# K^T V per head in 64-column tiles of TensorE instead of head pairs on the whole array

## The chip, the cores and the metric

The kernel runs on one core of a Trainium2 chip. The metric is device time of one execution in microseconds; the time before is the median of five runs, 145.91 us (145.01 to 146.12). TensorE multiplies matrices (in the profile PE for its matmuls and PEld for its weight loads), VectorE is DVE, ScalarE is ACT, GpSimd is POOL, and SyncE is SP, which here issues the loads and nearly all stores.

## What is computed

A gated linear attention is followed by a maxout feed-forward layer. In the reference, cut to what matters:

```python
batch, n_heads, seq, head_dim = (4, 8, 768, 48)
for t in range(S):
    state = alpha[:, :, t, :, None] * state + np.einsum('bhd,bhe->bhde', k[:, :, t], v[:, :, t])
    y[:, :, t] = np.einsum('bhd,bhde->bhe', q[:, :, t], state)
x = y.transpose(0, 2, 1, 3).reshape(B * S, H * D)     # 3072 tokens of 384
out = np.maximum(x @ w1, x @ w2) @ w_out              # d_ff = 1024
```

Inputs and output are float32. Each head's state is a 48 x 48 matrix.

## The kernel before

The sequence is cut into chunks of 128 steps, and two chunks of one batch element (256 tokens, all 8 heads) make a unit: 12 units, u = 0 to 11. Unit u works on batch element u % 4, so the state that unit u starts from comes from unit u - 4. Inside a chunk the recurrence is turned into matmuls. `ln` takes the logarithm of alpha on ScalarE (L193), `sumd` and `sumc` form running sums by matmul (L223, L237), `expm`, `expp` and `expd` exponentiate them, `kmul` and `qmul` scale k and q with the result into fp16 tiles `kn` and `qn` (L285 on GpSimd, L289 on VectorE). These tiles give each head 64 columns, of which 48 hold data and 16 are zero. `turn` transposes kn and qn (L296, evacuated at L303); `pmm` forms the scores of each head (L345, tile `pp`), `pmask` masks them (L351, tile `pt`); `ystate` and `yin` add the state's part and the chunk's own part of y (L369, L381); `xturn` transposes y (L397). The feed-forward part of a unit runs one unit later: `hid` (L410, relu at L415) and `outx`, `outg` (L429, L435, evacuated at L439). It uses max(a, b) = b + relu(a - b), with w1 - w2 and w2 times w_out formed once near the start. `dummies` (L504) are matmuls on zeros in the first part.

The change is in two small functions. `kvmm(u, cc)` forms K^T V of chunk cc for all heads on TensorE. It takes a pair of heads at a time: the 128 columns of two heads of kn are the stationary operand, and the 96 columns of the same two heads of v are streamed (L318). The result in PSUM is 128 x 96 for each pair, of which only the two 48-column blocks on the diagonal are wanted. Units 0 and 1 (`PAIRED`) keep the steps of a chunk in half of the partitions, and need two matmuls of 64 rows that add up (L312). `kvsum(u, cc)` then adds the decayed state `sb` to the two wanted blocks on VectorE, one half of the partitions at a time (L331), or copies them where no state exists yet (L333). Its result `tm` goes to `state`, where GpSimd multiplies it with the decay into the next `sb` (L277).

The instructions' order on each engine is written by hand (`manual_schedule`), and each engine runs its queue in order. For units 2 to 11 the loop body orders TensorE's work so:

```python
kvmm(u, 0); pmm(u, 0)          # then kvsum, pmask, state on other engines
if more(u): kvmm(u, 1)         # u + 4 < 12, so units 2 to 7
hid(u - 1, 0); hid(u - 1, 1); sumd(u + 1); hid(u - 1, 2); sumc(u + 1)
pmm(u, 1); ystate(u); hid(u - 1, 3, True)
outp(u - 1, 0); yin(u); turn(u + 1, 0); turn(u + 1, 1)
outx(u - 1, 1); xturn(u); outg(u - 1, 1)
```

The work ahead of a unit's first kvmm is thus `outg` (L435) of the unit before. Loads of unit u + 4 stand at the head of the body on SyncE's queue, in buffers of four.

Of the kernel before, what the change touches and what calls it, by code (L numbers as in the profile page):

```python
# [9 lines left out]
FP32 = mybir.dt.float32  # L10
# [5 lines left out]
def kernel(  # L16
# [27 lines left out]
    nc = tc.nc  # L44
    B, H, S, D = q.shape
    C = 128
    HP = H // 2
# [7 lines left out]
    PAIRED = (0, 1)  # L55
# [63 lines left out]
    for n in range(2):  # L119
        f = slice(n * NF // 2, (n + 1) * NF // 2)  # L120
        nc.sync.dma_start(out=wof[:, f], in_=moe_w_out.rearrange("(s p) d -> p s d", p=128)[:, f])  # L121
    for n in range(4):
        f = slice(n * DFF // 4, (n + 1) * DFF // 4)
# [8 lines left out]
    for cc in range(2):  # L132
        r = slice(64 * cc, 64 * cc + 64)
        for j in range(2):
            nc.gpsimd.affine_select(
                out=mc[r, j], in_=mc[r, j], compare_op=ALU.is_ge, fill=0.0, base=-j,
                pattern=[[1, 2], [2, 64]], channel_multiplier=-2,
            )
        r = slice(64 * cc, 64 * cc + 32)
# [4 lines left out]
    for cc in range(2):  # L144
        r = slice(64 * cc, 64 * cc + 64)
# [19 lines left out]
    for j in range(2):  # L165
        r = slice(64 * j, 64 * j + 64)
        nc.gpsimd.affine_select(
            out=um[r], in_=um[r], compare_op=ALU.is_ge, fill=0.0, base=-j,
# [14 lines left out]
    def pair(t, j):  # L183
        return t[:, 2 * j : 2 * j + 2, :].rearrange("p h w -> p (h w)")

    def new(tag, shape, dtype, bufs, name):
        return psp.tile(shape, dtype, tag=tag, bufs=bufs, name=name)


    def ln(u):  # L190
        X = st[u]
        X["lg"] = LG[u % NB]
        nc.scalar.activation(  # L193
            out=X["lg"][:, :, :, 0:D], in_=X["af"].rearrange("p h j d -> p j h d"), func=ACTF.Ln
        )

    def vcast(u):
        X = st[u]

        X["v16"] = gp.tile([128, 3, H, D], FP16, tag="v16", name="v16")  # L200
        for cc, j in ((0, 0), (1, 1), (0, 1), (1, 0)):
            o = X["v16"][64 * j : 64 * j + 64, cc]
            i = X["vf"][64 * cc : 64 * cc + 64, :, j, :]
            if cc == j:
                nc.gpsimd.tensor_copy(out=o, in_=i)  # L205
            else:
                nc.scalar.copy(out=o, in_=i)  # L207
                if u in PAIRED:
                    nc.gpsimd.tensor_copy(out=X["v16"][64 * cc : 64 * cc + 64, 2], in_=i)
# [93 lines left out]
            nc.vector.tensor_copy(out=X["qk"][:, cc], in_=tp.rearrange("p n h t -> p (n h) t"))  # L303

    def kvmm(u, cc):
        X = st[u]
        X["kvp", cc] = kvp = new(f"g{3 - cc}", [128, HP, 2 * D], FP32, 1, "kv")
        for j in range(HP):
            if u in PAIRED:
                r = slice(64 * cc, 64 * cc + 64)  # L310
                for i in range(2):
                    nc.tensor.matmul(  # L312
                        kvp[:, j, :], lhsT=pair(X["kn"][i][r], j),
                        rhs=X["v16"][r, cc if i == cc else 2, 2 * j : 2 * j + 2, :],
                        start=(i == 0), stop=(i == 1),
                    )
            else:
                nc.tensor.matmul(  # L318
                    kvp[:, j, :], lhsT=pair(X["kn"][cc], j), rhs=X["v16"][:, cc, 2 * j : 2 * j + 2, :],
                    start=True, stop=True,  # L320
                )

    def kvsum(u, cc):
        X = st[u]
        tm = X[f"tm{cc}"] = gp.tile([128, HP, D], FP32, tag=f"tm{cc}", bufs=6 if cc else 3, name="tm")
        kvp = X["kvp", cc]
        for a in range(2):
            r = slice(64 * a, 64 * a + 64)
            e = slice(D * a, D * a + D)
            if ("sb", cc) in X:  # L330
                nc.vector.tensor_add(out=tm[r], in0=kvp[r, :, e], in1=X["sb", cc][r])  # L331
            else:
                nc.vector.tensor_copy(out=tm[r], in_=kvp[r, :, e])  # L333

    def more(u):
        return u + B < NU
# [190 lines left out]
    dummies(1)  # L527
    wturn(0)
    kvmm(0, 0)
    kvmm(0, 1)  # L530
    kvsum(0, 0)
    state(0, 1)
    load(2)
    pmm(0, 1)
    pmask(0, 1)
    kvsum(0, 1)
    dummies(2)
    wturn(1)
# [41 lines left out]
    ln(2)  # L580
    outp(0, 0)
    kvmm(1, 0)
    kvmm(1, 1)
    kvsum(1, 0)
    state(1, 1)
    kvsum(1, 1)
# [102 lines left out]
```

## Time and profile before

| | |
|---|---|
| median of five runs | 145.91 us (145.01 to 146.12) |
| the profiled execution | 146.12 us, span 144.4 us |
| granted TensorE clock | 1.00 |
| TensorE busy | 134.8 us (93%), 1689 matmuls |
| weight loads | 97.0 us (67%), 1689 |
| ScalarE, VectorE, GpSimd busy | 96.6 (67%), 87.5 (61%), 56.6 us (39%) |
| HBM | 23.59 MB read, 4.72 MB written, 196 GB/s over the span |
| matmuls of kvmm | 64 of 128x96 (L318), 32 of 64x96 (L312) |
| VectorE operations of kvsum | 32 adds (L331), 8 copies (L333), 64x192 each |

A busy time is the sum over instructions of one engine within the span. Matmuls are pipelined, and the profile gives each of them its whole latency (206 ns for a kv matmul of 96 columns), so their spacing is read from the chain of waits: it follows the work that ended last back from the end, and gives each piece the time from its start to the start of the next. A line of the chain reads: start in us, length in us, engine, tile and line, number of instructions. A line of a group reads: line, engine, operation, out<-in, shapes and number, then busy us and mean ns, then the engine's idle time before it and what ended it.

### The profile page before, as it was taken

The page shows a single profiled execution, that of the slowest core. Times are in us where ns is not written, and L with a number is a line of the kernel's source. Part 1 is how long each engine was busy: PE and PEld are TensorE (multiplying, and loading weights), DVE is VectorE, ACT ScalarE, POOL GpSimd, SP SyncE. Part 2 cuts the span into 40 slices and gives each one's busy share as a digit, 9 for nine tenths or more (in the row PEclk, how much of TensorE's full clock was granted, in tenths as well). Part 3 has the DMA queues.
Part 4 walks back from the last instruction along what each step waited for, and adds up shares of the span by engine and source line. Part 5 has one row for each costly group of instructions (what it writes and reads, how often), then busy time and mean ns, then how long its engine had stood idle before and what let it go on. Part 6 is the DMA issues. An engine that isn't in the chain of part 4 may idle for free.

```text
span 144.4 us, 4259 instructions
## 1 busy us (share of the span) xinstructions
PE 134.8 (93%) x1689; PEld 97.0 (67%) x1689; DVE 87.5 (61%) x180; ACT 96.6 (67%) x200; POOL 56.6 (39%) x111
## 2 busy tenths in 40 slices
PE   6868879998999999999999999999999999999991
PEld 2335545755867677777877777678777777776770
DVE  6048883855966757765767777566676765671110
ACT  3467732498587686789686976786869767655530
POOL 7491542056424346173191371641913716410000
PEclk9999999999999999999999999999999999999999
DMA  4999999969959979999799999979959979020203
GB/s 113 270 371 309 305 368 346 241 126 211 198 102 250 138 142 300 159 216 186 160 293 140 283 202 215 241 133 269 197 97 294 207 136 370 0 109 5 109 0 109
DMA packets 76483, 28.58 MB, mean 198 GB/s; under 512 B 71728, under 2 KB 74672, under 8 KB 76464
## 3 DMA queue, kind: packets, MB, share of 16 engines
q1 hardware_dynamic: 76320, 28.22, 86.0%
q8 instruction: 13, 0.21, 0.7%
q10 hardware_dynamic: 144, 0.10, 0.2%
q14 instruction: 6, 0.05, 0.1%
HBM read 23.59 MB, written 4.72 MB: 196 GB/s over the span
## 4 chain that ended last, share of the span: by engine, by line
PE 64%; SPq 22%; DMA 8%; ACT 2%; issue 1%; DVE 0%; ACTq 0%
PE hp L410 19%; PE op L435 17%; SPq L75 10%; DMA af<-in_alpha_dram 8%; PE op L429 7%; SPq L85 5%; PE tp L296 5%; PE pp L345 3%; SPq L124 3%; PE cs L237 3%; PE ya L381 2%; PE xp L397 2%; PE kv L318 2%; SPq L115 2%; SPq L121 1%
## 5 line engine op out<-in xcount | busy, mean ns | idle before, releaser
L410 PE MATMUL hp<-xt,w 128*128 128x256 f16 x288 | 37.7, 273 | 0.7 <-ACT outs L439 0.2
L415 ACT ACTIVATE gT<-hp 128x512 f16<-128x512 f32 x47 | 27.9, 597 | 14.8 <-PE hp L410 14.3
L351 DVE TENSOR_TENSOR pt<-pp,um 128x512 f16<-128x512 f32 x48 | 30.9, 686 | 10.7 <-PE pp L345 10.4
L435 PE MATMUL op<-wo,gT 128*128 128x384 f16 x184 | 34.0, 326 | 0.0
L285 POOL TENSOR_TENSOR kn<-kf,Em 128x384 f16<-128x384 f32 x24 | 23.4, 996 | 25.7 <-ACT Em L247 25.7
L410 PEld LDWEIGHTS <-w 128*128 128x128 f16 x288 | 25.9, 97 | 5.9 <-issue 1.4
L435 PEld LDWEIGHTS <-gT 128*128 128x128 f16 x184 | 17.5, 98 | 10.5
L277 POOL TENSOR_TENSOR sb<-tm,dd 128x192 f16<-128x192 f32 x20 | 10.1, 506 | 30.9 <-DVE tm L331 22.9
L289 DVE TENSOR_TENSOR qn<-qf,cs 128x384 f16<-128x384 f32 x24 | 12.3, 551 | 12.8 <-ACT de L257 11.9
L439 ACT COPY outs<-op 128x384 f32<-128x384 f32 x23 | 10.9, 476 | 13.0 <-PE op L435 12.9
L331 DVE TENSOR_TENSOR tm<-kv,sb 64x192 f32<-64x192 f32 x32 | 11.3, 353 | 8.8 <-PE kv L318 7.9
L205 POOL CAST v<-vf 64x384 f16<-64x384 f32 x24 | 12.0, 501 | 9.0 <-DMA vf<-in_v_dram 8.0
L303 DVE COPY qk<-tp 128x1024 f16<-128x1024 f16 x20 | 12.9, 686 | 4.3 <-PE tp L296 4.3
L429 PE MATMUL op<-w2o,xt 128*128 128x384 f16 x69 | 15.0, 326 | 0.0
L193 ACT ACTIVATE lg<-af 128x768 f16<-128x768 f32 x12 | 10.1, 843 | 6.1 <-DMA af<-in_alpha_dram 5.9
L207 ACT CAST v<-vf 64x384 f16<-64x384 f32 x24 | 12.2, 510 | 2.5 <-DMA vf<-in_v_dram 2.0
L247 ACT ACTIVATE Em<-cs 128x384 f32<-128x384 f32 x24 | 11.6, 485 | 2.5 <-PE cs L237 2.5
L252 ACT ACTIVATE cs<-cs 128x384 f32<-128x384 f32 x24 | 11.8, 494 | 0.0
L504 PE MATMUL warm<-wz 128*128 128x512 f16 x30 | 9.9, 442 | 1.3 <-DVE halves L149 1.3
L388 ACT CAST xn<-ya 128x384 f16<-128x384 f32 x24 | 10.4, 492 | 0.0
L296 PE MATMUL tp<-ident,kn 128*128 128x128 f16 x96 | 9.3, 218 | 1.0 <-DVE qn L289 0.5
L345 PE MATMUL pp<-qk 48*128 48x128 f16 x192 | 9.8, 217 | 0.4 <-DVE qk L301 0.4
(66 smaller groups left out, 155.2 us busy)
## 6 DMA issues: line engine op xcount, KB each, us to landing
af<-in_alpha_dram SPq DMA_DIRECT2D x12, 384.0 KB, 5.7
vf<-in_v_dram SPq DMA_DIRECT2D x12, 384.0 KB, 4.7
out_dram<-outs SPq DMA_DIRECT2D x11, 384.0 KB, 4.4
kf<-in_k_dram SPq DMA_DIRECT2D x40, 96.0 KB, 4.6
qf<-in_q_dram SPq DMA_DIRECT2D x40, 96.0 KB, 4.0
w2f<-in_moe_w_dram SPq DMA_DIRECT2D x3, 512.0 KB, 5.9
wof<-in_moe_w_out_dram SPq DMA_DIRECT2D x2, 768.0 KB, 8.2
w1f<-in_moe_w_dram SPq DMA_DIRECT2D x4, 384.0 KB, 9.3
```

Source lines behind the costliest of these rows:

```text
L75: nc.sync.dma_start(out=t[name].rearrange("p h j d -> p h (j d)"), in_=rows(src, u, 0, 2 * C).rearrange("h (p j) d -> p h (j d)", j=2),)
L207: nc.scalar.copy(out=o, in_=i)
L285: nc.gpsimd.tensor_mul(out=X["kn"][cc][:, :, 0:D], in0=part(u, "kf", cc), in1=X["Em"][cc])
L289: nc.vector.tensor_mul(out=X["qn"][cc][:, :, 0:D], in0=part(u, "qf", cc), in1=X["csv"][cc])
L296: nc.tensor.transpose(tp[:, n, j, :], pair(src, j), ident)
L303: nc.vector.tensor_copy(out=X["qk"][:, cc], in_=tp.rearrange("p n h t -> p (n h) t"))
L345: nc.tensor.matmul(pa[a][:, j, :], lhsT=qk[r, 1, j, :], rhs=qk[r, 0, j, :], start=True, stop=True)
L351: nc.vector.tensor_mul(out=pt[:, a], in0=X["pa", cc][a], in1=um.unsqueeze(1).to_broadcast([128, HP, C]))
L410: nc.tensor.matmul(hp[:, n, :], lhsT=w12[:, ds, f * 128 : (f + 1) * 128], rhs=X["xt"][:, ds].rearrange("p n t -> p (n t)"), start=(ds == 0 ...
L415: nc.scalar.activation(out=gT[:, 2 * f2 : 2 * f2 + 2, :], in_=hp, func=ACTF.Relu)
L429: nc.tensor.matmul(op, lhsT=X["xt"][:, ds, n, :], rhs=w2o[:, ds, :], start=(ds == 0), stop=False)
L435: nc.tensor.matmul(op, lhsT=X["gT"][:, f, n * C : (n + 1) * C], rhs=wo16[:, f, :], start=False, stop=(f == NF - 1))
```

## The change

Each head gets its own matmul: the 64 columns of kn of one head are stationary, the 48 columns of v of the same head are streamed. The result of an even head goes to PSUM partitions 0 to 63, that of an odd head to 64 to 127, side by side in a tile of 64 columns of the array each. The PSUM tile has 48 instead of 96 columns for a pair, and holds only wanted values, so that one VectorE operation over 128 partitions takes the place of two over 64.

```diff
-        X["kvp", cc] = kvp = new(f"g{3 - cc}", [128, HP, 2 * D], FP32, 1, "kv")
+        X["kvp", cc] = kvp = new(f"g{3 - cc}", [128, HP, D], FP32, 1, "kv")
         for j in range(HP):
-            if u in PAIRED:
-                r = slice(64 * cc, 64 * cc + 64)
-                for i in range(2):
+            for i in range(2 if u in PAIRED else 1):
+                for a in range(2):
+                    h = 2 * j + a
+                    if u in PAIRED:
+                        r = slice(64 * cc, 64 * cc + 64)
+                        lhsT, rhs = X["kn"][i][r, h, :], X["v16"][r, cc if i == cc else 2, h, :]
+                    else:
+                        lhsT, rhs = X["kn"][cc][:, h, :], X["v16"][:, cc, h, :]
                     nc.tensor.matmul(
-                        kvp[:, j, :], lhsT=pair(X["kn"][i][r], j),
-                        rhs=X["v16"][r, cc if i == cc else 2, 2 * j : 2 * j + 2, :],
-                        start=(i == 0), stop=(i == 1),
+                        kvp[64 * a : 64 * a + 64, j, :], lhsT=lhsT, rhs=rhs,
+                        start=(i == 0), stop=(i == 1 or u not in PAIRED),
                     )
-            else:
-                nc.tensor.matmul(
-                    kvp[:, j, :], lhsT=pair(X["kn"][cc], j), rhs=X["v16"][:, cc, 2 * j : 2 * j + 2, :],
-                    start=True, stop=True,
-                )
...
         tm = X[f"tm{cc}"] = gp.tile([128, HP, D], FP32, tag=f"tm{cc}", bufs=6 if cc else 3, name="tm")
-        kvp = X["kvp", cc]
-        for a in range(2):
-            r = slice(64 * a, 64 * a + 64)
-            e = slice(D * a, D * a + D)
-            if ("sb", cc) in X:
-                nc.vector.tensor_add(out=tm[r], in0=kvp[r, :, e], in1=X["sb", cc][r])
-            else:
-                nc.vector.tensor_copy(out=tm[r], in_=kvp[r, :, e])
+        if ("sb", cc) in X:
+            nc.vector.tensor_add(out=tm, in0=X["kvp", cc], in1=X["sb", cc])
+        else:
+            nc.vector.tensor_copy(out=tm, in_=X["kvp", cc])
```

## Prediction

> **What bounds the kernel now.** I began with the page's busy table, then the chain of waits in order of time, then the busy time by stretches, then the groups of the lines that the change touches. The busy table and one stretch:
>
> ```profile
> PE 134.8 (93%) x1689; PEld 97.0 (67%) x1689; DVE 87.5 (61%) x180; ACT 96.6 (67%) x200; POOL 56.6 (39%) x111
> 78.00:88.00 10.00, 10.00 (x145) 7.66 (x142) 6.94 (x14) 7.75 (x17) 4.28 (x8) 1.00 1.06 210
> ```
>
> The columns of the second line are the stretch, its length, PE, PEld, DVE, ACT and POOL busy with counts, the clock, DMA share and GB/s. TensorE is busy throughout, at clock 1.00, while VectorE works 6.94 of 10 us. A busy TensorE need not be a full one, so the chain has to say whether it waits (start, us, engine and line):
>
> ```profile
> 87.54 0.17 PE kv L318 x4
> 87.71 0.33 PE pp L345 x8
> 88.03 0.28 PE kv L318 x4
> 88.31 1.31 PE hp L410 x12
> 89.62 0.18 PE cs L223 x8
> 89.80 0.68 PE hp L410 x6
> 90.47 0.43 PE cs L237 x4
> 90.91 0.23 PE pp L345 x8
> 91.13 0.20 PE ya L369 x16
> 91.33 0.76 PE hp L410 x6
> ...
> 93.88 0.40 PE ya L381 x16
> ...
> 97.30 0.17 PE kv L318 x4
> 97.47 0.33 PE pp L345 x8
> 97.80 1.42 PE hp L410 x12
> ```
>
> Each piece starts where the one before ends. From 49.79 us to the last evacuation at 141.30 the chain is TensorE alone but for one 0.61 us activation near the end. One unit with two kv groups lasts 97.30 - 87.54 = 9.76 us. So a change in TensorE's own time counts in full there, and VectorE time does not. Earlier it is different:
>
> ```profile
> ACT lg L193 <- DMA af<-in_alpha_dram: 5.9, 5, 2.4
> 48.50:58.00 9.50, 9.32 (x124) 7.01 (x119) 6.64 (x13) 7.31 (x16) 4.33 (x8) 1.00 0.92 197
> ```
>
> Until 48.53 us the chain runs through SyncE's DMA issues and the landings of alpha. The logarithms start at 39.27, 48.53 and 58.26 us, each after a wait for alpha; the one at 48.53 holds the next activation back, and TensorE stands still for 0.3 us until 49.79. Waits for alpha end with the one at 58.26.
>
> **VectorE part.** Forty half-height operations become twenty full ones. The rows:
>
> ```profile
> L331 DVE TENSOR_TENSOR tm<-kv,sb 64x192 f32<-64x192 f32 x32 | 11.3, 353 | 8.8 <-PE kv L318 7.9
> L289 DVE TENSOR_TENSOR qn<-qf,cs 128x384 f16<-128x384 f32 x24 | 12.3, 551 | 12.8 <-ACT de L257 11.9
> ```
>
> From 192 to 384 elements the time rises by 198 ns, about 1.03 ns an element; 128 more elements (the 128x512 pt at 686 ns) add 135 ns, the same slope. The 64-partition row lies on the line of the 128-partition rows, so height is free and the new operation should take the same 0.35 us. Twenty times 0.353 = 7.1 us leave VectorE. On the path this is worth nothing after 49.79 us, since no TensorE piece there waits for tm or for the pt that follows it; the state product on GpSimd, which does wait for tm, is ready 0.35 us sooner and waits longer for its next input. Before that TensorE waits once for tm (0.3 us at L369), but the next logarithm waits for alpha anyway. I cost it at zero; uncovered, that wait would return 0.3 us.
>
> **TensorE part: which groups are on the path.** The 16 unpaired kv groups are two in each unit 2 to 7 and one in each unit 8 to 11. Those of units 2 and 3 (starts 37.74 to 48.61 us) lie ahead of the stand before 49.79 us, whose 0.3 us can cover them. Units 4 to 11 start at 58.02 and later: 4 x 2 + 4 x 1 = 12 groups count.
>
> **TensorE part: the stream.** A group is now 4 matmuls of 96 columns, 0.17 us (42 ns each). It becomes 8 of 48 columns, with 8 weight loads of 64 columns instead of 4 of 128. No row shows column tiles. Lower bound: L369 runs 48-column matmuls two at a time in two row tiles, 16 in 0.20 us, so 8 in 0.10, or -0.07 us a group. If the two column tiles do not overlap, L381 is the row: 48-column matmuls on the whole array, 16 in 0.40 us, so 8 in 0.20, or +0.03. Above that, a weight load may be left in the open. All loads in the trace have 128 columns and are recorded at 92 to 98 ns, hidden behind matmuls at their best. Exposed once per pair they give 4 x 0.097 = 0.39 us, +0.22; exposed one by one 8 x 0.097 = 0.78, +0.61. The nearest row is L369 (two tiles, the same 48 columns), but its loads are of the wide kind, so I move away from it and take 0.17 us: no gain, no loss in the stream. Twelve groups: 0, between 12 x -0.07 = -0.84 and 12 x 0.22 = +2.6 us, at the very worst 12 x 0.61 = +7.3.
>
> The Trainium skill, "TensorEngine Tiling (Array Packing)", Restrictions, says that column tiling disables the fast weight load, and "TensorE: Matmul & The Clock Gate", LDWEIGHTS, gives a load as its columns divided by 1.2 in ns; as an estimate from that page 64 columns are 53 ns, hence 0.21 us a group with the tiles' loads side by side, and the total would be 0.5 us above mine, while its Part 3 promises overlap of column tiles. No run here shows a narrow load.
>
> **TensorE part: changing the array's shape.** This is the term that the diff does not show. The page's forms give L345, L369 and L237 48 or 64 rows, the others 128. Wherever the chain passes between the kinds, a piece is longer than its twin that comes from its own kind: pp after the full-height kv 0.33 against 0.23 after cs (+0.10); kv after pp 0.28 against 0.17 (+0.11); hp x12 after pp 1.42 against 1.31 after kv (+0.11); hp x6 after ya 0.76 against 0.68 (+0.08). So 0.10 us a change of shape. The Trainium skill, "TensorEngine Tiling (Array Packing)", Key Properties, says that changing the tiling mode drains the array, which agrees with these 0.08 to 0.11 us for row tiles; no run here shows it for columns.
>
> In the built instruction order the kv matmuls carry tiles of 128 rows by 64 columns, at columns 0 and 64. In a two-group unit the order is op, kv, pp, kv, hp. Before, op to kv and kv to hp were the same shape; the two changes were around pp. After, all four borders change shape: two more. In units 8 to 11 (op, kv, pp, hp) only op to kv is new: one more. On the path 4 x 2 + 4 x 1 = 12 additional changes. Bounds: 0 if column tiles change shape freely; 0.11, the dearest row, if they are like row tiles; I take 0.10, because the same array has to empty. 12 x 0.10 = +1.2 us. Units 0, 2 and 3 have 1 + 2 + 2 = 5 more changes, under the alpha loads; without that cover +0.5 us.
>
> **Waits and queues.** No wait moves: the orders of ScalarE, GpSimd and SyncE are unchanged, VectorE's only merges pairs, and the kv matmuls keep their place. What is behind a slower kv group is everything on TensorE; what is behind a faster tm is the pt operation, off the path. No DMA is added.
>
> **Sum.** VectorE 0, stream 0, shape +1.2 us. The profiled execution took 146.12 us, of which 144.4 is span and 1.7 lies around it; it becomes 147.3. It was the slowest of the five runs, 0.2 above the median of 145.91, so the median should come to 147.1, +0.8%.
>
> **Rivals.** *The pairs pay and the change of shape is free (faster).* If two column tiles run as L369's row tiles do (0.10 us) and a border to a column tile costs nothing, the sum is -0.84 us: 145.1, -0.6%. For it: L369 and L345 really run in pairs. Against it: four independent borders in the chain cost 0.08 to 0.11 us. It decides once the border costs under 0.01 us with pairs at 25 ns each; with borders at 0.07 the two cancel. *Narrow loads in the open (much slower).* With one exposed load per pair, +2.6 + 1.2 = +3.8: 149.7. For it: no row shows a load of 64 columns. Against it: TensorE hides nearly all loads today, and the row-tile pairs keep 25 ns. *It does nothing that can be seen.* If pairs gain 0.07 and borders cost 0.10, the net is 12 x 0.03 = +0.4 us, 146.3. *VectorE's release matters:* only before 49.79 us, at most the 0.3 us named above.
>
> **How the numbers follow.** A measurement of this kernel can tell about 0.5%, 0.73 us, from no change. My forecast, borders at 0.10 and a stream within 0.05 us of today's a group, has 0.52; its own range is 146.5 to 147.7, and 0.13 of the 0.52 falls inside 0.5%, 0.39 above. The narrow loads have 0.21, all slower. The free borders have 0.23, of which 0.20 is faster by over 0.5% and 0.03 is not. Nothing to be seen has 0.04. Faster 0.20; same 0.13 + 0.03 + 0.04 = 0.20; slower 0.39 + 0.21 = 0.60. The range leaves out the better part of the free borders (below 145.2) and the dearer half of the narrow loads (above 149.0), about 0.1 on each side.
>
> **What would show it.** In the chain after: the first hp x12 after a kv group at about 1.42 instead of 1.31 (border), the first kv piece after op longer by 0.10, a two-group unit at 9.96 us and a one-group unit at 9.69 instead of 9.59. VectorE's tm group at x16 and about 353 ns, its busy time down by 7 us. kv matmuls in pairs that start together mean overlap; starts evenly 25 ns apart, none; gaps of 50 ns or more between pairs mean exposed loads. I am wrong if units are shorter than 9.7 us, if they exceed 10.2, or if TensorE starts to wait for another engine after 50 us.

## The result and the profile after

The changed kernel takes 147.29 us (median of 43 runs, 146.12 to 149.04) against 146.02 us before (80 runs, 144.85 to 148.05). The ratio is 1.0078 with a 95% interval of 1.0062 to 1.0094: about 1.14 us slower, 0.9 to 1.4 by the interval. The ratios here and below compare the fast runs alone, those within 1.5% of the fastest run of their kernel, so a ratio can differ from that of the medians. The forecast was 147.1 us, +0.8%.

The profiled execution after took 147.60 us, with a span of 145.9 us. Its busy table (TensorE, weight loads, VectorE, ScalarE, GpSimd):

```profile
PE 136.5 (94%) x1785; PEld 96.7 (66%) x1785; DVE 79.5 (55%) x160; ACT 96.2 (66%) x200; POOL 56.6 (39%) x111
```

There are 96 more matmuls and 20 fewer VectorE operations; VectorE is 8.0 us less busy and the kernel is slower all the same. The chain of waits after, its start behind the alpha load and then the same unit as before (start, us, engine and line):

```profile
50.55 0.81 PE hp L406 x6
...
88.64 0.24 PE kv L318 x8
88.88 0.33 PE pp L341 x8
89.20 0.24 PE kv L318 x8
89.44 1.42 PE hp L406 x12
...
98.54 0.24 PE kv L318 x8
...
108.20 0.24 PE kv L318 x8
```

From the chain before, the start and the first kv of unit 9, which the prediction did not show (its 97.30 is unit 8's):

```profile
49.79 0.81 PE hp L410 x6
...
106.89 0.17 PE kv L318 x4
```

From one unit's first kv to the next it is now 98.54 - 88.64 = 9.90 us with two groups (9.76 before), and 108.20 - 98.54 = 9.66 with one (106.89 - 97.30 = 9.59 before, 9.60 in the next unit). I call a change of the array's shape between two pieces a border. The first kv piece went from 0.17 to 0.24, and the first hidden-layer piece (hp) after kv from 1.31 to 1.42: these two pieces carry the new borders. The second kv piece had a border before and went from 0.28 to 0.24. Everything else in the unit is as it was. Over units 4 to 11 this makes 4 x 0.14 + 4 x 0.065 = 0.82 us. (In these two executions it is 0.76, because one hp piece before, in unit 4, took 1.38 instead of 1.31.)

The groups of the two changed lines and of a load that kept its shape, after (busy us, mean ns | idle before):

```profile
L327 DVE TENSOR_TENSOR tm<-kv,sb 128x192 f32<-128x192 f32 x16 | 5.7, 354 | 9.1 <-PE kv L318 8.4 <-POOL sb L277 0.7
L318 PEld LDWEIGHTS <-kn 128*64 128x64 f16 x128 | 3.3, 110 | 3.8 <-issue 1.6 <-ACT lg L193 1.0 <-ACT v L207 0.6
L341 PEld LDWEIGHTS <-qk 48*128 48x128 f16 x192 | 6.3, 94 | 3.3 <-DVE qk L301 0.8 <-issue 0.7
```

A full-height VectorE operation takes what a half-height one took (354 against 353 ns). The two changed groups account for 7.0 of VectorE's 8.0 us. The narrow weight loads are recorded at 110 ns, longer than the wide ones at 94, although they move half the columns; so the recorded length does not tell what a load costs.

The spans differ by 1.5 us, of which the units explain half. The other 0.76 lies ahead of 51 us: the TensorE part of the chain starts at 50.55 instead of 49.79 us, after an alpha load. The experiments had to tell which part of this belongs to the change.

### The profile page after: what moved, and what is told of

Read it like the earlier page. It is cut to its first block, busy times and chain, and to the rows that moved or that the text cites. A ratio compares the mean times of both kernels' runs of the same rounds, so it can differ in the third digit from the quotient of the medians.

```text
span 145.9 us, 4430 instructions
## 1 busy us (share of the span) xinstructions
PE 136.5 (94%) x1785; PEld 96.7 (66%) x1785; DVE 79.5 (55%) x160; ACT 96.2 (66%) x200; POOL 56.6 (39%) x111
## 4 chain that ended last, share of the span: by engine, by line
PE 64%; SPq 22%; DMA 8%; ACT 2%; issue 1%; DVE 0%; ACTq 0%
PE hp L406 19%; PE op L431 17%; SPq L75 10%; DMA af<-in_alpha_dram 8%; PE op L425 6%; SPq L85 5%; PE tp L296 5%; PE pp L341 3%; SPq L124 3%; PE cs L237 3%; PE ya L377 2%; PE xp L393 2%; PE kv L318 2%; SPq L115 2%; SPq L121 1%
## 5 line engine op out<-in xcount | busy, mean ns | idle before, releaser
L327 DVE TENSOR_TENSOR tm<-kv,sb 128x192 f32<-128x192 f32 x16 | 5.7, 354 | 9.1 <-PE kv L318 8.4
L384 ACT CAST xn<-ya 128x384 f16<-128x384 f32 x24 | 10.4, 492 | 0.0
L296 PE MATMUL tp<-ident,qn 128*128 128x128 f16 x96 | 9.3, 219 | 0.9 <-DVE qn L289 0.9
```

The source lines that it names most:

```text
L296: nc.tensor.transpose(tp[:, n, j, :], pair(src, j), ident)
```

## Experiments

Theory: TensorE pays for changes of the array's shape, and little else moves. Rivals: the loss arises in the start or in the loads; it is the number of matmuls; VectorE matters; the tiles don't overlap.

**Tiles in units 4 to 11 alone.** `kvmm` and `kvsum` of the changed kernel for `u >= B`, those of the kernel before otherwise.

> Column tiles and the single VectorE operation in units 4 to 11 only, units 0 to 3 as before. Theory of the borders (each change between array shapes costs 0.09 to 0.10 us, the pairs win back a little): all of the steady part's loss, 4 x 0.14 + 4 x 0.065 = 0.8 us, so a ratio of 1.0055 against before, and the same unit lengths as the changed kernel (9.90 and 9.66 us). Rival (the loss arises before 50 us, in the alpha loads or in the start): no difference that can be told, under 0.2 us, in which case the unit lengths would have to be made up elsewhere.

Measured: 147.18 us, ratio 1.0069 (1.0040 to 1.0098). The units are 9.90 us long with two groups and 9.67 with one (starts at 88.45, 98.35 and 108.02 us in the chain). The rival that puts the whole loss ahead of 50 us falls: the late part alone gives 1.0 us, with an interval (0.6 to 1.4) that holds the expected 0.8.

**Tiles in units 0 to 3 alone, run twice.** The same with `u < B`.

> Column tiles and the single VectorE operation in units 0 to 3 only, units 4 to 11 as before. Theory of the borders with cover by the alpha loads: at most 0.3 us, ratio 1.000 to 1.002, units 9.76 and 9.60 us long. Rival (start): 0.4 to 0.8 us of loss, ratio 1.003 to 1.005, with the first chain piece of the steady part starting later than 49.8 us in the profile.

> The kernel with tiles and the single VectorE operation in units 0 to 3 only, once more; the first time it came out 1.5% above before, with alpha late in every unit from 58 us on. Theory A (the load stream needs about as long per unit as TensorE, 9.8 to 10 us, and by chance ran late that time): ratio 1.000 to 1.005, and alpha waits of ScalarE after 65 us gone or smaller. Theory B (the tiles in the early units set the load stream back each time): ratio 1.010 to 1.020 again, with alpha waits of 0.5 to 1.5 us in every unit.

Measured: 1.0152 (1.0087 to 1.0217) the first time and 1.0066 (1.0024 to 1.0108) the second. All six runs of the first time lie between 147.37 and 150.01 us (median 149.55, before 146.16), the twelve of the second between 145.46 and 150.20 (median 147.66, before 145.90). Both miss what the theory of the borders expected, and the second lies between theories A and B. The profile shows where it went. The chain of the first run, in the steady part, where the chain before had TensorE alone (SPq is SyncE's issue of a DMA, DMA the time until the load lands):

```profile
97.42 1.56 PE hp L442 x12
...
99.00 0.61 ACT gT L447
99.61 0.35 SPq L475
...
100.01 6.78 DMA af<-in_alpha_dram
...
106.82 0.84 ACT lg L193
```

The units themselves are 9.76 us long when they run (77.39 to 87.15 us), but alpha for a later unit lands at 106.8 us and the logarithm starts at that moment. In the second run it is a load of q:

```profile
107.10 0.17 PE kv L318 x4
...
118.55 5.54 DMA qf<-in_q_dram
...
127.52 0.17 PE kv L318 x4
```

From 107.10 to 127.52 are two one-group units, 20.42 us instead of 19.19. At the first kv of unit 8, with all the tiles done, neither profiled run had lost more than 0.2 us against the chain before (96.92 and 97.50 us, 97.30 before). So the loads, which the prediction had done with at 58 us, can bound the kernel after 100 us too. Whether the early tiles cause that or only meet it, these two runs don't tell; the light loads below were made for it.

**VectorE's part alone.** Whole-array matmuls as before, and one addition over 128 partitions. The kernel leaves out the odd heads' own blocks: it takes the even head's 48 columns for both halves.

```diff
-        for a in range(2):
...
-                nc.vector.tensor_add(out=tm[r], in0=kvp[r, :, e], in1=X["sb", cc][r])
...
+            nc.vector.tensor_add(out=tm, in0=X["kvp", cc][:, :, 0:D], in1=X["sb", cc])
```

> Matmuls as before, but one VectorE operation over 128 partitions that takes the even head's 48 columns for both halves (the odd heads' own block is left out). Theory: VectorE is off the path, ratio 1.000 within 0.2%, tm at 16 operations of 0.355 us, VectorE busy down by 7 to 8 us. Rival (VectorE's release matters before 50 us): faster by up to 0.3 us, ratio 0.998. If a wider VectorE operation disturbed others: slower.

Measured: ratio 0.9981 (0.9946 to 1.0015); VectorE 79.5 us busy, units 9.76 us. No difference can be told: what the change takes off VectorE is worth at most 0.8 us by the interval, and nothing by the units.

**Twice the matmuls without tiles.**

```diff
-                nc.tensor.matmul(
-                    kvp[:, j, :], lhsT=pair(X["kn"][cc], j), rhs=X["v16"][:, cc, 2 * j : 2 * j + 2, :],
-                    start=True, stop=True,
-                )
+                for a in range(2):
+                    nc.tensor.matmul(
+                        kvp[:, j, D * a : D * a + D], lhsT=pair(X["kn"][cc], j), rhs=X["v16"][:, cc, 2 * j + a, :],
+                        start=True, stop=True,
+                    )
```

> As before, but each unpaired kv group as 8 matmuls of 48 columns with the two heads' 128 columns stationary (whole array, no tiles, twice the matmuls). Theory: no change of shape is added, a group takes 8 x 25 ns = 0.20 instead of 0.17 us, +0.03 x 12 = +0.4 us, ratio 1.0025. Rival (it is the number of matmuls that costs, not the tiles): as much as the changed kernel, +0.8 to +1.1 us.

Measured: ratio 1.0037 (0.9998 to 1.0077). The twelve runs go from 145.78 to 151.19 us, with a median of 148.23, so the time decides nothing, but the chain is clear:

```profile
86.30 1.30 PE op L436 x8
87.60 0.20 PE kv L319 x8
87.80 0.33 PE pp L346 x8
88.13 0.30 PE kv L319 x8
88.44 1.31 PE hp L411 x12
```

Eight matmuls of 48 columns on the whole array take 0.20 us, 25 ns each, and the piece after them stays at 1.31. The number of matmuls costs 0.03 us a group; the 0.11 in hp needs the tiles. The scatter of the runs does not need them, since this kernel has no column tiles.

**The heads in another order.** The loop over `a` outside, so that the four even heads come first.

```diff
-        for j in range(HP):
-            for i in range(2 if u in PAIRED else 1):
-                for a in range(2):
+        for a in range(2):
+            for j in range(HP):
+                for i in range(2 if u in PAIRED else 1):
```

> The changed kernel with the heads in another order: the four even heads first, then the four odd ones, so that neighbouring matmuls lie in the same column tile. Theory (two column tiles work at the same time when neighbours lie in different tiles): the group loses the overlap, 8 starts 25 to 55 ns apart instead of 4 pairs 32 ns apart, so 0.1 to 0.3 us more a group, 12 groups, +1.2 to +3.6 us against the changed kernel, ratio against before 1.016 to 1.033. Rival (column tiles do not overlap, only the issue order makes pairs): within 0.3 us of the changed kernel, ratio 1.008.

Measured: ratio 1.0106 (1.0064 to 1.0148). My expectation failed. The chain:

```profile
88.12 0.25 PE kv L318 x8
88.37 0.33 PE pp L341 x8
88.70 0.25 PE kv L318 x8
88.94 1.42 PE hp L406 x12
```

A group takes 0.25 us instead of 0.24. In the trace the eight matmuls of a group start at 0, 13, 52, 65, 84, 97, 115 and 129 ns; in the changed kernel's order at 0, 3, 52, 56, 84, 87, 116 and 119. Starts 13 ns apart can't both be in a tile that takes 32 ns for each, so the two tiles work at once here too, although four neighbours in the program lie in the same tile. The rival is wrong as well: the overlap is real, and with four of one tile in a row it does not hang on the order. With eight in a row it does. In units 0 and 1 of this kernel, whose tiles are 64 x 64, eight matmuls of one tile follow one another, and the trace shows the first starts at 0, 53, 85, 116, 148 and 154 ns: five of the first tile, and only then, 6 ns behind the fifth, the first of the second tile. (Which start belongs to which tile is read from the program's order.) From the first to the last start of their 32 matmuls it is 703 ns, against 403 in the changed kernel's order.

**The two kv groups side by side.** `kvmm(u, 1)` moved ahead of `pmm(u, 0)`.

> The changed kernel with the second kv group moved directly behind the first, ahead of the scores. Theory of the borders: a two-group unit has three added and old borders instead of four, so 0.09 to 0.10 us less a unit for units 4 to 7, unit length 9.80 instead of 9.90 us, and 0.4 us less in all, ratio against before 1.005; the second kv group is 0.13 us long. Rival (each kv group costs more by itself, whatever lies beside it): unit length 9.90 us, ratio 1.008.

Measured: ratio 1.0082 (1.0049 to 1.0114). The chain of this kernel:

```profile
87.29 0.36 PE kv L318 x16
87.66 0.33 PE pp L341 x8
87.99 1.42 PE hp L406 x12
...
97.08 0.24 PE kv L318 x8
```

The unit is 97.08 - 87.29 = 9.79 us, 0.11 less than 9.90: one border less. And it separates the two terms: the second group, with no border ahead, adds 0.36 - 0.24 = 0.12 us. That is the stream of a tiled group; the other 0.12 of the first group is its border. The gain of 4 x 0.11 us in the units can't be read in the time: its interval just holds the expected 1.005, and 1.008 as well.

**Tiles with VectorE in halves.** The addition in two operations of 64 partitions.

> The changed kernel's matmuls with VectorE taking the compact result in two operations of 64 partitions again. Theory (VectorE is off the path): the changed kernel's time, ratio against before 1.006 to 1.010, unit lengths 9.90 and 9.66 us, 40 operations of 0.35 us. Rival (the merged VectorE operation gives part back): slower than the changed kernel by 0.3 us or more.

Measured: ratio 1.0116 (1.0073 to 1.0158), units 9.90 and 9.66 us (89.05, 98.95, 108.62 in the chain). The interval overlaps the changed kernel's. The profiled run is 0.41 us later than the changed kernel's at unit 7 (89.05 against 88.64) and 0.42 at unit 9, so what it lost lies ahead of these units. The units say that VectorE is off the path there, the time alone leaves it open.

**Weights of 48 columns.** The zero columns are left away, and VectorE and GpSimd take the 48 rows of each half.

```diff
-                        lhsT, rhs = X["kn"][cc][:, h, :], X["v16"][:, cc, h, :]
+                        lhsT, rhs = X["kn"][cc][:, h, 0:D], X["v16"][:, cc, h, :]
-                        kvp[64 * a : 64 * a + 64, j, :], lhsT=lhsT, rhs=rhs,
+                        kvp[64 * a : 64 * a + D, j, :], lhsT=lhsT, rhs=rhs,
```

> The changed kernel with 48 instead of 64 columns of weights for each head (the zero columns left away), and VectorE and GpSimd taking the 48 wanted rows of each half in two operations. Theory (the 32 ns between pairs is the load of 64 columns, about half a ns a column): pairs 25 to 27 ns apart, a group 0.22 instead of 0.24 us, units 9.86 and 9.64 us, ratio against before 1.006. Rival (32 ns is a fixed spacing of column tiles): pairs 32 ns apart, units 9.90 and 9.66 us.

Measured: a group takes 0.21 us, with pairs 25 ns apart instead of 32; the units are 9.85 and 9.63 us. The chain, and the group of loads:

```profile
87.40 0.21 PE kv L320 x8
...
88.16 1.42 PE hp L410 x12
...
97.25 0.21 PE kv L320 x8
...
106.88 0.21 PE kv L320 x8
```

```profile
L320 PEld LDWEIGHTS <-kn 128*48 128x48 f16 x128 | 2.8, 100 | 3.8 <-issue 2.2 <-ACT lg L193 0.6 <-ACT v L207 0.3
```

The moving data are the same 48 columns, so at 64 columns it is the width of the weights that sets the 32 ns. That it is their load, as I expected, fits but is not shown by itself: with the weights' columns the rows that a tile writes go from 64 to 48 too. At 48 columns the spacing is the 25 ns that 48 moving columns also take on the whole array (above). The whole time, ratio 1.0104 (1.0042 to 1.0166), does not show the 4 x 0.05 + 4 x 0.03 = 0.3 us that the units save.

**Lighter loads.** In three kernels (before, after, tiles in units 0 to 3) k and q of units 2 to 11 come by one DMA each with 384-byte rows. The kernels leave out the order of the steps, which arrive in another one than the computation needs; the instructions of the compute engines are the same:

```diff
-            load_kq(u, 0)
-            load_kq(u, 1)
+            for name, src in (("kf", k), ("qf", q)):
+                x = st[u][name] = ldp.tile([128, 2, H, D], FP32, tag=name, name=name)
+                nc.sync.dma_start(
+                    out=x.rearrange("p j h d -> p (j h d)").rearrange("p (h x) -> p h x", h=H),
+                    in_=rows(src, u, 0, 2 * C).rearrange("h (p j) d -> p h (j d)", j=2),
+                )
```

> The kernel before with lighter loads: k and q of units 2 to 11 are taken by one DMA each in rows of 384 bytes instead of four DMAs each in rows of 192 bytes, so that the steps arrive in another order than the computation needs (that order is left out; every instruction on the compute engines is the same). This takes the load stream off the edge. Theory (TensorE alone bounds the steady part): unit lengths 9.76 and 9.60 us as before, alpha waits after 58 us gone; the first 50 us get shorter, by 1 to 5 us. Rival (loads matter throughout): units shorter than 9.7 us.

> The changed kernel with the same lighter loads. Theory of the borders alone: 0.8 to 1.1 us more than the kernel before with lighter loads (twelve groups at 0.065 to 0.07, and with the cover of the loads gone four more groups and one border), the spread of the runs narrower than that of the changed kernel. Rival (the changed kernel loses a further 0.3 to 0.5 us by the load stream): the same 0.8 us here, but 1.2 us or more with the heavy loads. Rival (tiles cost something that the steady units don't show): 1.3 us or more here too.

> Tiles and the single VectorE operation in units 0 to 3 only, with the same lighter loads. Theory (the loss of the early tiles came from late loads): 0 to 0.4 us more than the kernel before with lighter loads (four groups at 0.07 and one border, uncovered). Rival (the early tiles cost TensorE or VectorE time that the unit lengths don't show): 0.7 us or more.

Measured, with the range of 12 runs each: pairs 144.96 us (144.80 to 145.26), tiles 146.06 (145.71 to 146.41), early tiles 145.24 (144.92 to 145.45). With the same bytes in 55,043 packets instead of 76,483 the runs of each kernel agree within 0.7 us; 29 runs of the kernel before, made along with them, go from 144.99 to 146.91. Late tiles cost 146.06 - 145.24 = 0.82 us, as the units say. Early tiles cost 145.24 - 144.96 = 0.28 us (0.23 at the first kv of unit 4 in the two chains, 57.69 against 57.46), near two groups in each of units 2 and 3 at 0.07; their ranges overlap, so this difference is the less certain one. Together 1.10 us. With pairs the second kv piece of unit 4 starts at 57.96 instead of 58.68 us, so the start gained 0.7 us, not the 1 to 5 that I expected, and the units are still 9.76 us (67.73, 77.49, 87.25). The chain of tiles with lighter loads shows the early groups on the path:

```profile
37.93 0.24 PE kv L322 x8
...
47.73 0.24 PE kv L322 x8
...
57.53 0.24 PE kv L322 x8
```

These are 9.80 us apart, since TensorE no longer stands still for alpha there; ScalarE's waits for alpha are these, after with its own loads and then with the lighter ones (us, times, longest):

```profile
ACT lg L193 <- DMA af<-in_alpha_dram: 6.3, 8, 2.5
```

```profile
ACT lg L197 <- DMA af<-in_alpha_dram: 2.8, 2, 2.3
```

## Why the prediction was right, and where it was not

**Borders: right, size included.** I took 0.10 us for each of 12 added changes of shape, by the row-tile rows. Two groups side by side saved 0.11 us a unit, the border ahead of a kv group is 0.12, and hp after a tile is 1.42, the same as after the row tiles. The Trainium skill, "TensorEngine Tiling (Array Packing)", Key Properties, says that a change of tiling mode drains the array; the runs here agree for column tiles, at about 0.11 us.

**Stream: mis-sized.** I took 0.17 us, no gain. It is 0.12, near the lower bound of 0.10: the tiles overlap, and only the 64 columns of weights keep a pair at 32 ns instead of 25. So the late part is 12 groups at 0.065 to 0.07, 0.82 us, not 1.2. (One reading beside this sum was off: the loads of `dummies` are recorded at 111 ns, so not all lie between 92 and 98. The sum doesn't use it.)

The Trainium skill, "TensorE: Matmul & The Clock Gate", LDWEIGHTS, gives a load as its columns divided by 1.2 in ns, as an estimate 53 ns for 64 columns; the pairs here are 32 ns apart with 64 columns and 25 with 48, so the measurement decides. Part 3 of that page, by which small matmuls in tiles run concurrently in the array, agrees with the two tiles here, whose matmuls start 3 ns apart.

**Cover: mis-sized, the other way.** I costed units 0 to 3 at zero and named 0.5 us without the cover. Uncovered they cost about 0.28, since the stream's gain comes off their borders too. Were they covered? The whole is 1.14 us (0.9 to 1.4) with heavy loads and 1.10 with light ones, so nothing of the 0.28 can be seen to have been hidden. The two errors are of opposite sign, 1.2 + 0 against 0.82 + 0.3. That they nearly cancel is luck, and it is why 147.1 came so near to 147.29.

**VectorE: right.** Its two groups lost 11.3 + 2.8 - 5.7 - 1.4 = 7.0 us, 7.1 predicted, and its part alone cannot be told from nothing.

**"Waits for alpha end at 58 us": wrong.** It held in the one execution that I read. After, ScalarE waited for alpha at 78.32, 88.10 and 97.75 us again, for 0.3 to 0.65 us, without holding TensorE up; in the early-tile runs waits for alpha and q set the end.

**Rivals.** The free borders fall: the border costs 0.11. Narrow loads in the open fall: 32 ns a pair. A change that can't be seen falls too: the interval starts at 0.6%. What stays open is why early tiles with heavy loads lost 0.7 and 1.5% when the same tiles lost 0.2% (145.24 against 144.96) with light ones. That it goes through late loads is shown, that the tiles cause the lateness is not. Two things keep it open: the kernel with twice the matmuls and no column tiles scattered as widely, and the light runs were made on another chip than either heavy run.

No version of the tiles beats the kernel before. Tiles of 48 columns (9.85 us a two-group unit) and groups side by side (9.79) both stand above its 9.76. The two together were not tried; by these numbers they would come to about 9.74 there and stay at 9.63 instead of 9.60 in one-group units, which cancels.

## What to carry to other kernels

Before tiles of the array are used for small matmuls, count the borders: here each change between whole array, row tiles and column tiles took 0.08 to 0.12 us, which two overlapping tiles of four matmuls each, gaining 0.05, could not pay back. Groups of the same shape belong side by side, and operations saved on an engine that nobody waits for are no gain. When the chain of one execution names a single engine, look also at how near the loads come to it: here lighter loads shrank the scatter of the runs and let a difference of 0.3 us be read.

## What the runs showed that I had not expected

The two column tiles overlap even where four neighbouring matmuls of the program lie in the same tile: pairs still start 13 ns apart and follow each other after 32 ns. With eight neighbours in one tile the second tile waits until the fifth has started. The spacing of the pairs goes from 32 ns to 25 when the columns of the weights go from 64 to 48 and the moving data stay the same. And the load stream, with 192-byte rows, needs about as long for a unit as TensorE does: before, alpha loads were issued 8.8 to 10.4 us apart after 50 us, with units of 9.6 to 9.8 us, the last at 108.36 us. With 384-byte rows for k and q, and units of the same length, the last was issued at 87.70.
